# Softmax sums on four column groups at once, two pairs summed by the vector engine, filler matmuls at the start and moved weight steps in an attention and mixing kernel

## The chip, the cores and the metric

The kernel runs on one core of a Trainium2 chip. A core has a matmul engine (PE, with its weight loads shown as PEld), a vector engine (DVE), a scalar engine (ACT), GpSimd (POOL) and a queue engine that issues the transfers here (SP). The metric is the device time of one execution in microseconds; of several runs the median counts, and less is better. Instruction times come from a profile of one execution.

## The reference

For each of 8 batches, softmax attention with a soft cap over 12 heads of 64 channels and 448 positions, and then a mixing layer on the 768 channels:

```python
scores = scale * np.matmul(q, k.transpose(0, 1, 3, 2))
scores = cap * np.tanh(scores / cap)
scores = scores - np.max(scores, axis=-1, keepdims=True)
attn = np.exp(scores)
attn = attn / (np.sum(attn, axis=-1, keepdims=True) + 1e-09)
x = np.matmul(attn, v)           # heads side by side: (8, 448, 768)

theta = x @ w_theta
zr, zi = x * np.cos(theta), x * np.sin(theta)
u = x + einsum(w_tok_r, zr) + einsum(w_tok_i, zi)
out = u + np.maximum(u @ w_ch, 0.0)
```

All arrays are float32. Where the cap is at most 64 the kernel leaves out the maximum (the branch that runs here); the other branch, `general`, is in the program and is not taken.

## The kernel before

**Pairs and stages.** Two heads make a pair, so a batch has 6 pairs and the program 48. It goes through stages `s`. Stage `s` computes the scores of pair `s` in two halves (`qk_half`: 448 keys as four blocks of 112 rows, two blocks to a half), each half followed on ACT by a tanh (L195) and later by an exponential in place (`exp_half`, L201). In the same stage the pair before, `k = s - 1`, is multiplied by its values (`av`, L233), copied out by ACT (L236), and its exponentials are summed over the keys (`sums`). Every second pair the sums are inverted (`invert`, a DVE reciprocal, L275) and spread over the rows by transfers; two or three stages later `norm` multiplies the attention output by them.

**Sums.** The sum over keys is a matmul with a block of ones 32 columns wide (`sum_pair`, L248), so that each head of two pairs has 32 rows of one PSUM tile `r`: rows 0 and 32 for the even pair, 64 and 96 for the odd one. Pairs below `DIRECT = 10` sum all four blocks on PE, pair by pair. For later pairs DVE adds the four blocks first (`add_half`, L223 and L226), and PE sums the result of both pairs in one go.

**Buffers.** The scores have one PSUM tile of four banks, so the next half's scores wait for the tanh of this half. All else on PE shares four tiles of one bank each (tag "m"): attention output, sums, theta, transposes, mixing and channel results, one after another.

**First stages.** Stages 0 to 7 (`FIRST = 8`) have attention alone, and beside it the weights are prepared: each 128-row piece of `w_theta` (th), `w_tok` (tk) and `w_ch` (ch) is loaded (`>th2`), scaled on ACT (`*th2`, L101) and split by seven DVE instructions into a rounded part and a rest (`th2`, L106 to L115; for ch pieces the copy into the rounded part is ACT's, L111). The table `WEIGHTS` says after which step of which stage each word stands. The th and ch pieces share two staging buffers `g_sb0` and `g_sb1`, which theta uses later too. ch pieces 2 to 5 are prepared in stages 11 to 13.

**Later stages.** From stage 8 on each group of six stages, parts 0 to 5, also runs one batch of the mixing layer by `part_scripts`: theta (L299 to L301), sine and cosine, rotation (L323), transposes on PE (`transp`, L332, with the split of the result on ACT, L333, and DVE, L334), mixing over positions (`mix`, L341 to L343), and the channel product (`chan`). In float32r three products replace one, with split operands `xs`, `us`, `zh` and `zl`. From pair 14 on (`WHOLE`) the scores use split operands too, made by `prep` on DVE (L178, L179) one stage ahead.

**Order.** Nothing is scheduled by a tool: every engine works through its instructions in the order in which the code issues them, and semaphores hold an instruction until its operands are there and its output's buffer is free. SP issues the transfers in program order as well, and one that waits holds up those behind it.

Of the kernel before, what the change touches and what calls it, by code (L numbers as in the profile page):

```python
# [28 lines left out]
DIRECT = 10  # L29
# [5 lines left out]
def softcap_attn_then_spectral_mix(ctx, tc, qk2, v, cap, w_theta, w_tok, w_ch, ident, outT):  # L35
# [47 lines left out]


    class Split:
# [14 lines left out]
        def scale(self):  # L100
            nc.scalar.activation(self.hw, self.hw, AF.Copy, scale=2.0**-112)  # L101

# [136 lines left out]
    def sum_pair(k, r, halves=(0, 1)):  # L239

        if k in pst:
            addends = [(pst.pop(k), True, True)]
        else:
            addends = [(pt[k, c // 2][:, c % 2], c == 0, c == NCH - 1) for c in range(NCH) if c // 2 in halves]
        for a, start, stop in addends:
            for hh in range(2):
                i = 2 * (k % 2) + hh
                nc.tensor.matmul(r[32 * i : 32 * i + 32, :S], ones_sb, a[:, hh, :], start=start, stop=stop)  # L248

    def sums(k, halves=(0, 1)):  # L250

        direct = k < DIRECT or state["general"]
# [4 lines left out]
        if direct:
            if state["general"] and 0 not in halves:
                return
            sum_pair(k, state["r"], halves)  # L260
        else:
            sum_pair(k - 1, state["r"])
            sum_pair(k, state["r"])
# [223 lines left out]
```

## Time and profile before

| | |
|---|---|
| median of 3 runs | 981.16 us (980.04 to 984.58) |
| the profiled execution, time | 981.55 us |
| its span, first to last instruction | 979.7 us |
| PE busy | 953.9 us, 97% of the span |
| DVE busy, ACT busy | 631.6 us, 597.4 us |
| mean granted PE clock | 0.995 |
| stage 8's first theta matmul starts | 96.68 us |

The span leaves out 1.85 us before the first and after the last instruction. "PE busy" counts from a matmul's start to its modelled end, and matmuls overlap; so 97% says that PE seldom stands still, not that it works at its peak. A float32 matmul of the program shows as two records in the trace (float32r ones and transposes as one), so 8 records of scores are four matmuls of the program. In a timeline a row gives the start, the time from the first start to the last end of the records that it merges, the engine, the line, the operation, output and inputs, the count, and in brackets the idle time before it with what ended that.

### The profile page before, as it was taken

The page shows a single profiled execution, that of the slowest core. Times are in us where ns is not written, and L with a number is a line of the kernel's source. Part 1 is how long each engine was busy: PE and PEld are TensorE (multiplying, and loading weights), DVE is VectorE, ACT ScalarE, POOL GpSimd, SP SyncE. Part 2 cuts the span into 40 slices and gives each one's busy share as a digit, 9 for nine tenths or more (in the row PEclk, how much of TensorE's full clock was granted, in tenths as well). Part 3 has the DMA queues.
Part 4 walks back from the last instruction along what each step waited for, and adds up shares of the span by engine and source line. Part 5 has one row for each costly group of instructions (what it writes and reads, how often), then busy time and mean ns, then how long its engine had stood idle before and what let it go on. Part 6 is the DMA issues. An engine that isn't in the chain of part 4 may idle for free.

```text
span 979.7 us, 12717 instructions
## 1 busy us (share of the span) xinstructions
PE 953.9 (97%) x5192; PEld 693.5 (71%) x5192; DVE 631.6 (64%) x865; ACT 597.4 (61%) x615; POOL 0.4 (0%) x6
## 2 busy tenths in 40 slices
PE   6999999989999999999999999999999999999997
PEld 2333667657787787777677767876877777789897
DVE  5788665885865658557676567665586566763541
ACT  5887676466954677555876469636784567642520
POOL 0000000000000000000000000000000000000000
PEclk9999999999999999999999999999999999999999
DMA  6654221322102211032111321122211330102001
GB/s 221 196 186 127 66 69 39 121 98 85 48 29 76 79 54 48 30 104 76 38 48 36 106 67 46 49 68 75 66 48 29 86 93 29 29 1 76 1 1 60
DMA packets 30739, 68.68 MB, mean 70 GB/s; under 512 B 4304, under 2 KB 16720, under 8 KB 30672
## 3 DMA queue, kind: packets, MB, share of 16 engines
q1 hardware_dynamic: 30672, 67.78, 22.7%
q8 instruction: 43, 0.70, 0.3%
q14 instruction: 24, 0.20, 0.1%
HBM read 45.74 MB, written 11.01 MB: 58 GB/s over the span
## 4 chain that ended last, share of the span: by engine, by line
PE 78%; DVE 10%; ACT 9%; DMA 2%; issue 1%; SPq 0%; DVEq 0%
PE a L233 13%; PE s L193 12%; PE mx L341 6%; PE mx L342 6%; PE mx L343 6%; PE ch L299 6%; PE ch L301 6%; PE ch L300 6%; PE th L299 4%; PE th L300 4%; PE th L301 4%; PE r L248 3%; ACT p L195 3%; PE t L332 3%; DVE ri L275 2%; ACT p L201 1%
## 5 line engine op out<-in xcount | busy, mean ns | idle before, releaser
L195 ACT ACTIVATE p<-s,qscale 112x1792 f32<-112x1792 f32 x96 | 168.7, 1757 | 171.2 <-PE s L193 171.1
L201 ACT ACTIVATE p<-p,cap_sb 112x1792 f32<-112x1792 f32 x96 | 170.6, 1790 | 0.5
L233 PE MATMUL a<-p,v 112*64 112x448 f32 x768 | 155.5, 547 | 0.0
L341 PE MATMUL mx<-wtk_h,zh 128*128 128x448 f32 x336 | 126.3, 376 | 1.8 <-DVE zl L334 1.8
L342 PE MATMUL mx<-wtk_l,zh 128*128 128x448 f32 x336 | 122.9, 366 | 0.0
L343 PE MATMUL mx<-wtk_h,zl 128*128 128x448 f32 x336 | 122.9, 366 | 0.0
L233 PEld LDWEIGHTS a<-p,v 112*64 112x64 f32 x768 | 51.0, 137 | 87.9 <-issue 78.5
L299 PE MATMUL ch<-us,wch_h 128*128 128x448 f32 x288 | 107.2, 372 | 0.0
L299 PE MATMUL th<-xs,wth_h 128*128 128x448 f32 x288 | 106.9, 371 | 0.0
L301 PE MATMUL ch<-us,wch_l 128*128 128x448 f32 x288 | 105.6, 367 | 0.0
L300 PE MATMUL ch<-us,wch_h 128*128 128x448 f32 x288 | 105.5, 366 | 0.0
L300 PE MATMUL th<-xs,wth_h 128*128 128x448 f32 x288 | 105.4, 366 | 0.0
L301 PE MATMUL th<-xs,wth_l 128*128 128x448 f32 x288 | 105.3, 366 | 0.0
L226 DVE TENSOR_TENSOR ps<-ps,p 112x896 f32<-112x896 f32 x76 | 82.7, 1088 | 1.3
L275 DVE RECIPROCAL ri<-r 128x448 f32<-128x448 f32 x24 | 70.9, 2954 | 14.8 <-PE r L248 14.8
L312 DVE SCALAR_TENSOR_TENSOR g_sb<-g_sb 128x448 f32<-128x448 f32 x48 | 30.0, 624 | 72.6 <-ACT g_sb L311 72.2
L334 DVE TENSOR_TENSOR zl<-t,zh 128x512 fp32r<-128x512 f32 x96 | 55.2, 617 | 24.9 <-ACT zh L333 24.9
L341 PEld LDWEIGHTS mx<-wtk_h,zh 128*128 128x128 f32 x336 | 63.2, 188 | 7.7 <-DVE zl L334 3.0
L352 DVE SCALAR_TENSOR_TENSOR x<-ch,x 128x448 f32<-128x448 f32 x48 | 29.8, 621 | 59.0 <-PE ch L301 59.0
L343 PEld LDWEIGHTS mx<-wtk_h,zl 128*128 128x128 f32 x336 | 63.1, 188 | 5.3
L342 PEld LDWEIGHTS mx<-wtk_l,zh 128*128 128x128 f32 x336 | 63.2, 188 | 4.8
L344 DVE TENSOR_TENSOR x<-mx,x 128x448 f32<-128x448 f32 x48 | 29.9, 623 | 52.9 <-PE mx L343 52.3
(71 smaller groups left out, 1411.6 us busy)
## 6 DMA issues: line engine op xcount, KB each, us to landing
qk_sb<-in_qk SPq DMA_DIRECT2D x35, 448.0 KB, 3.3
v<-in_v SPq DMA_DIRECT2D x48, 224.0 KB, 2.5
bc<-ri SPq DMA_DIRECT2D x96, 112.0 KB, 2.3
out_dram<-x SPq DMA_DIRECT2D x48, 224.0 KB, 2.0
qk<-in_qk SPq DMA_DIRECT2D x13, 448.0 KB, 3.3
g_sb<-in_wth SPq DMA_DIRECT2D x6, 768.0 KB, 5.1
g_sb<-in_wch SPq DMA_DIRECT2D x6, 768.0 KB, 5.3
swk_raw<-in_wtok SPq DMA_DIRECT2D x7, 448.0 KB, 4.2
```

The source lines that it names most:

```text
L193: nc.tensor.matmul(sp[:CP, i, hh, :S], kk[k][rows, 1, ks], qq[k][rows, 0, :], start=n == 0, stop=n == len(products) - 1)
L195: nc.scalar.activation(pp, sp[:CP, :, :, :S], AF.Tanh, scale=qscale[:CP])
L201: nc.scalar.activation(pp, pp, AF.Exp, scale=cap_sb[:CP])
L226: nc.vector.tensor_tensor(pst[k], pst[k], pt[k, 1][:, i], op=ALU.add)
L233: nc.tensor.matmul(acc[hh * D : (hh + 1) * D, :S], va[:, hh, c, :], pt[k, c // 2][:, c % 2, hh, :], start=c == 0, stop=c == NCH - 1)
L275: nc.vector.reciprocal(ri, r[:, :S])
L299: nc.tensor.matmul(acc[:, :S], wh[:, j, ms], t[:, 0, :], start=j == 0, stop=False)
L300: nc.tensor.matmul(acc[:, :S], wh[:, j, ms], t[:, 1, :], start=False, stop=False)
L301: nc.tensor.matmul(acc[:, :S], wl[:, j, ms], t[:, 0, :], start=False, stop=j == NJ - 1)
L341: nc.tensor.matmul(acc[:, :S], zh[:, c, :], wtk_h[:, c, :], start=c == 0, stop=False)
L342: nc.tensor.matmul(acc[:, :S], zh[:, c, :], wtk_l[:, c, :], start=False, stop=False)
L343: nc.tensor.matmul(acc[:, :S], zl[:, c, :], wtk_h[:, c, :], start=False, stop=c == NC2 - 1)
```

## The change

**Fillers.** A new `fill(n)` issues n matmuls of the ones block with itself, 112 columns each, into a PSUM tile that nobody reads. 8 stand ahead of the branch on the cap, 2 ahead of the first scores, 8 between the two halves of stage 0 and 10 behind them.

**Sums of the first batch.** For pairs 0 to 5 the sums of an even pair are no longer issued in its own stage; they are issued with those of the odd pair after it, block by block, so that matmuls for all four row groups of `r` stand next to each other. The exponentials of an even pair must live one stage longer: those of pairs 0, 2 and 4 get buffers of tag "xhl", which the split operands `xs` and `us` use later. For that `split_x` now takes one buffer for two of its operands (3 buffers twice as large in place of 6). Pairs 6 and 7 are summed as before.

**Pairs 8 and 9.** `DIRECT` goes from 10 to 8, so DVE adds the four blocks of these pairs, three instructions each, and PE sums them together in stage 10.

**Weight steps.** Pieces th0 to th3 and ch2 are scaled on DVE (`#`, `vscale`) and not on ACT; ch2's copy into the rounded part also goes to DVE. tk6 is split in stage 9 and not at the end of stage 8. ch2 is split early in stage 11, and the load of ch4 into the same buffer follows it there; the load of ch3 stays at the end of stage 11.

**Part 2.** In part 2 of every batch `invert` and `prep` move behind the first script entry, the transposes and the split of piece 1.

```diff
-DIRECT = 10
+DIRECT = 8
+
+FILL = {"before the branch": 8, "first scores": 2, "half": 8, "slot": 10}
...
+    def fill(n):
+
+        t = psM.tile([P, 512], F32, tag="m", name=f"fill{len(fills)}")
+        fills.append(t)
+        for _ in range(n):
+            nc.tensor.matmul(t[:32, :CP], ones_sb, ones_sb[:, :1].broadcast_to([CP, CP]), start=True, stop=True)
...
+        def vscale(self):
+            nc.vector.tensor_scalar_mul(self.hw, self.hw, 2.0**-112)
...
-            steps["ch", m] = Split(room_g(m), w_ch[m], wch_h[:, :, ms], wch_l[:, :, ms], True)
+            steps["ch", m] = Split(room_g(m), w_ch[m], wch_h[:, :, ms], wch_l[:, :, ms], m != 2)
...
-        (0, "a"): "*th0", (0, "b"): "th0 >th2", (0, "c"): "*th1 *tk0", (1, "b"): "tk0 >tk2 th1 >th3",
-        (2, "a"): "*th2", (2, "b"): "th2 >th4", (2, "c"): "*tk1", (3, "a"): "*th3", (3, "b"): "tk1 >tk3 th3 >th5",
+        (0, "a"): "#th0", (0, "b"): "th0 >th2", (0, "c"): "#th1 *tk0", (1, "b"): "tk0 >tk2 th1 >th3",
+        (2, "a"): "#th2", (2, "b"): "th2 >th4", (2, "c"): "*tk1", (3, "a"): "#th3", (3, "b"): "tk1 >tk3 th3 >th5",
...
-        (8, "b"): "tk5", (8, "c"): "*tk6 tk6 *ch1", (9, "a"): "ch1", (10, "c"): ">ch2", (11, "a"): "*ch2", (11, "c"): "ch2 >ch4 >ch3", (12, "b"): "*ch3 ch3 >ch5", (12, "c"): "*ch4 ch4", (13, "b"): "*ch5 ch5",
+        (8, "b"): "tk5", (8, "c"): "*tk6 *ch1", (9, "a"): "tk6 ch1", (10, "c"): ">ch2", (11, "a"): "#ch2 ch2 >ch4",
+        (11, "c"): ">ch3", (12, "b"): "*ch3 ch3 >ch5", (12, "c"): "*ch4 ch4", (13, "b"): "*ch5 ch5",
...
+    def apart(k):
+        return k < NP and k % 2 == 0
...
-        pp = pt[k, half] = wk.tile([CP, 2, 2, S], F32, tag="p", name=f"p{k}_{half}", bufs=3)
+        if apart(k):
+            pp = wk.tile([CP, 2, 2, S], F32, tag="xhl", name=f"p{k}_{half}", bufs=3)
+        else:
+            pp = wk.tile([CP, 2, 2, S], F32, tag="p", name=f"p{k}_{half}", bufs=3)
...
-        for a, start, stop in addends:
-            for hh in range(2):
-                i = 2 * (k % 2) + hh
-                nc.tensor.matmul(r[32 * i : 32 * i + 32, :S], ones_sb, a[:, hh, :], start=start, stop=stop)
+        for tiles, start, stop in addends:
+            for k, a in zip(ks, tiles):
+                for hh in range(2):
+                    i = 2 * (k % 2) + hh
+                    nc.tensor.matmul(r[32 * i : 32 * i + 32, :S], ones_sb, a[:, hh, :], start=start, stop=stop)
...
-        direct = k < DIRECT or state["general"]
+        alone = state["general"] or NP <= k < DIRECT
...
+        sum_pairs((k,) if alone else (k - 1, k), state["r"], halves)
...
-        t = wk.tile([P, 2, S], F32R, tag="xhl", name=f"{name}{b}_{j}", bufs=6)
+        if j % 2 == 0:
+            state["xhl"] = wk.tile([P, 2, 2, S], F32R, tag="xhl", name=f"{name}{b}_{j}", bufs=3)
+        t = state["xhl"][:, j % 2]
...
-                if not start:
+                if not start and part != 2:
                     invert(k)
...
-            if WHOLE <= s + 1 < NS:
+            if WHOLE <= s + 1 < NS and (start or part != 2):
                 prep(s + 1)
...
+                if part == 2 and i == 0 and not start:
+                    if 0 <= k < NS:
+                        invert(k)
+                    if WHOLE <= s + 1 < NS:
+                        prep(s + 1)
```

ACT in stages 0 and 1, up to the copy of the first attention output; `p0_0` is half 0 of pair 0, `g_sb0` holds th0, `g_sb1` th1 and `swk0_raw` tk0. Before:

```order
L195 ACTIVATE p0_0_121<-s0_0_120,qscale_70 112x1792
L101 ACTIVATE g_sb0_86<-g_sb0_86 128x768
L201 ACTIVATE p0_0_121<-p0_0_121,cap_sb_67 112x1792
L195 ACTIVATE p0_1_132<-s0_1_131,qscale_70 112x1792
L201 ACTIVATE p0_1_132<-p0_1_132,cap_sb_67 112x1792
L101 ACTIVATE g_sb1_87<-g_sb1_87 128x768
L101 ACTIVATE swk0_raw_114<-swk0_raw_114 128x448
L195 ACTIVATE p1_0_152<-s1_0_151,qscale_70 112x1792
L201 ACTIVATE p1_0_152<-p1_0_152,cap_sb_67 112x1792
L236 COPY x0_168<-a0_159 128x448
```

and with the change:

```order
L219 ACTIVATE p0_0_133<-s0_0_132,qscale_70 112x1792
L225 ACTIVATE p0_0_133<-p0_0_133,cap_sb_67 112x1792
L219 ACTIVATE p0_1_153<-s0_1_152,qscale_70 112x1792
L225 ACTIVATE p0_1_153<-p0_1_153,cap_sb_67 112x1792
L112 ACTIVATE swk0_raw_123<-swk0_raw_123 128x448
L219 ACTIVATE p1_0_184<-s1_0_183,qscale_70 112x1792
L225 ACTIVATE p1_0_184<-p1_0_184,cap_sb_67 112x1792
L260 COPY x0_200<-a0_191 128x448
```

The two scalings of th pieces are gone from ACT; that of tk0 stays.

PE from the attention output of pair 0 on to the sums of stage 2 (`a` is attention output, `r` sums, `s` scores; each row is a run of the program's matmuls). Before:

```order
L233 MATMUL a0_159<-p0_1_132,v0_110 64x448 x4
L248 MATMUL r0_172<-p0_0_121,ones_sb_83 32x448 x4
L193 MATMUL s1_1_177<-qk1_112 112x448 x4
L248 MATMUL r0_172<-p0_1_132,ones_sb_83 32x448 x4
L193 MATMUL s2_0_209<-qk2_138 112x448 x4
L233 MATMUL a1_218<-p1_0_152,v1_129 64x448 x4
L233 MATMUL a1_218<-p1_1_178,v1_129 64x448 x4
L248 MATMUL r0_172<-p1_0_152,ones_sb_83 32x448 x4
L193 MATMUL s2_1_235<-qk2_138 112x448 x4
L248 MATMUL r0_172<-p1_1_178,ones_sb_83 32x448 x4
```

and with the change:

```order
L257 MATMUL a0_191<-p0_1_153,v0_119 64x448 x4
L217 MATMUL s1_1_204<-qk1_121 112x448 x4
L217 MATMUL s2_0_232<-qk2_170 112x448 x4
L257 MATMUL a1_241<-p1_0_184,v1_150 64x448 x4
L257 MATMUL a1_241<-p1_1_205,v1_150 64x448 x4
L273 MATMUL r1_254<-p0_0_133,ones_sb_83 32x448 x2
L273 MATMUL r1_254<-p1_0_184,ones_sb_83 32x448 x2
```

Stage 1 has no sums; in stage 2 the two pairs alternate, two matmuls each: the last two rows come once more for the half's second block, and the same again for half 1 behind the scores.

DVE in part 2 of batch 1 (stage 16), where `ri15` is the inverse of the sums, `hi17` and `lo17` the split operands of the next scores, and `zl1_1` the split of the transposes of piece 1. Before:

```order
L323 TENSOR_TENSOR g_sb0_86<-g_sb0_86,x8_734 128x896
L275 RECIPROCAL ri15_1770<-r15_1765 128x448
L178 CAST hi17_1793<-qk_sb_85 128x896
L179 TENSOR_TENSOR lo17_1794<-qk_sb_85,hi17_1793 128x896
L334 TENSOR_TENSOR zl1_1_1799<-t1_1_0_1800,zh1_1_1798 128x512
L334 TENSOR_TENSOR zl1_1_1799<-t1_1_4_1807,zh1_1_1798 128x384
L344 TENSOR_TENSOR x6_534<-mx1_0_1815,x6_534 128x448
```

and with the change:

```order
L346 TENSOR_TENSOR g_sb0_86<-g_sb0_86,x8_760 128x896
L357 TENSOR_TENSOR zl1_1_1805<-t1_1_0_1806,zh1_1_1804 128x512
L357 TENSOR_TENSOR zl1_1_1805<-t1_1_4_1813,zh1_1_1804 128x384
L296 RECIPROCAL ri15_1819<-r15_1784 128x448
L193 CAST hi17_1827<-qk_sb_85 128x896
L194 TENSOR_TENSOR lo17_1828<-qk_sb_85,hi17_1827 128x896
L367 TENSOR_TENSOR x6_564<-mx1_0_1834,x6_564 128x448
```

The two splits stand ahead of the reciprocal and the casts.

More of the change, by code (lines that the diff above doesn't have):

```diff
@@ L78, in softcap_attn_then_spectral_mix @@
     g_sb = [const.tile([P, 3, 2, S], F32, name=f"g_sb{i}") for i in range(2)]
+    def fill(n):
[3 more added lines that the diff above has]
+            nc.tensor.matmul(t[:32, :CP], ones_sb, ones_sb[:, :1].broadcast_to([CP, CP]), start=True, stop=True)
+    fills = []
     def load_consts():
@@ L152, in weights @@
             step = steps[word[-3:-1], int(word[-1])]
-            {">": step.load, "*": step.scale}.get(word[0], step.split)()
+            {">": step.load, "*": step.scale, "#": step.vscale}.get(word[0], step.split)()
     hi, lo, vt, pt, pst, bc = {}, {}, {}, {}, {}, {}
@@ L181, in prep @@
             load_qk(k + 1)
+    def apart(k):
+        return k < NP and k % 2 == 0
     def qk_half(k, half):
         sp = psS.tile([P, 2, 2, 512], F32, tag="s", name=f"s{k}_{half}")
-        pp = pt[k, half] = wk.tile([CP, 2, 2, S], F32, tag="p", name=f"p{k}_{half}", bufs=3)
+        if apart(k):
+            pp = wk.tile([CP, 2, 2, S], F32, tag="xhl", name=f"p{k}_{half}", bufs=3)
+        else:
+            pp = wk.tile([CP, 2, 2, S], F32, tag="p", name=f"p{k}_{half}", bufs=3)
+        pt[k, half] = pp
         for i in range(2):
@@ L237, in av, with sum_pairs @@
         X[k // NP, k % NP] = x
-    def sum_pair(k, r, halves=(0, 1)):
-        if k in pst:
-            addends = [(pst.pop(k), True, True)]
-        else:
-            addends = [(pt[k, c // 2][:, c % 2], c == 0, c == NCH - 1) for c in range(NCH) if c // 2 in halves]
-        for a, start, stop in addends:
-            for hh in range(2):
-                i = 2 * (k % 2) + hh
-                nc.tensor.matmul(r[32 * i : 32 * i + 32, :S], ones_sb, a[:, hh, :], start=start, stop=stop)
+    def sum_pairs(ks, r, halves=(0, 1)):
+        if ks[0] in pst:
+            addends = [([pst.pop(k) for k in ks], True, True)]
+        else:
+            addends = [([pt[k, c // 2][:, c % 2] for k in ks], c == 0, c == NCH - 1) for c in range(NCH) if c // 2 in halves]
+        for tiles, start, stop in addends:
[3 more added lines that the diff above has]
+                    nc.tensor.matmul(r[32 * i : 32 * i + 32, :S], ones_sb, a[:, hh, :], start=start, stop=stop)
     def sums(k, halves=(0, 1)):
-        direct = k < DIRECT or state["general"]
-        if not direct and k % 2 == 0:
+        alone = state["general"] or NP <= k < DIRECT
+        if not alone and k % 2 == 0:
             return
-        if (k % 2 == 0 or not direct) and 0 in halves:
+        if state["general"] and 0 not in halves:
+            return
+        if (k % 2 == 0 or not alone) and 0 in halves:
             state["r"] = psM.tile([P, 512], F32, tag="m", name=f"r{k}")
[L257 to L263, printed above, removed]
+        sum_pairs((k,) if alone else (k - 1, k), state["r"], halves)
     def invert(k):
@@ L384, in pipeline @@
             start = s < FIRST
+            if s == 0:
+                fill(FILL["first scores"])
             if live:
                 qk_half(s, 0)
+            if s == 0:
+                fill(FILL["half"])
             if start:
@@ L404, in pipeline @@
                 qk_half(s, 1)
+            if s == 0:
+                fill(FILL["slot"])
             if 0 <= k and start:
@@ L441, in softcap_attn_then_spectral_mix @@
         steps[step].load()
+    fill(FILL["before the branch"])
     wide = nc.values_load(wide_cap[:1, :1], min_val=0, max_val=1)
```

## The prediction

> **What bounds the kernel now.** I read the page's busy shares first, then who waits for whom on PE (engine, line, what it waited for; us in total, times, longest), then the timeline of the stretches with waits.
>
> ```profile
> PE s L193 <- ACT p L195: 8.9, 10, 2.8
> PE s L193 <- DMA qk_sb<-in_qk: 5.3, 1, 5.3
> PE t L332 <- DVE zl L334: 4.6, 6, 0.8
> ```
>
> PE is busy nearly all the span (the table above), and these three rows are most of its idle time. So time goes only where PE gets less work, or where one of these waits goes. The second stretch to read is a plain early stage:
>
> ```profile
> 27.86 3.23 PE L233 MATMUL a<-p,v 112*64 112x448 f32 x16
> 31.02 1.70 PE L248 MATMUL r<-p,ones_sb 112*32 112x448 f32 x8
> 32.64 1.76 PE L193 MATMUL s<-qk 64*112 64x448 f32 x8
> 34.45 1.76 ACT L195 ACTIVATE p<-s,qscale 112x1792 f32<-112x1792 f32 x1 [1.82 <-PE s L193]
> 36.24 1.79 ACT L201 ACTIVATE p<-p,cap_sb 112x1792 f32<-112x1792 f32 x1
> 37.95 2.48 PE L233 MATMUL a<-p,v 112*64 112x448 f32 x12
> ```
>
> One stage lasts 10.09 us (27.86 to 37.95), and these rows are a closed loop: attention output, half the sums, second scores, tanh, exponential, and with that the next attention output. PE looks full, but a sum taken out behind the attention output shortens the loop by its whole 1.62 us (31.02 to 32.64); one taken out behind the second scores shortens nothing, as ACT works meanwhile.
>
> **A. The start, to stage 2's first scores (26.17).**
>
> ```profile
> 5.30 3.17 PE L193 MATMUL s<-qk_sb 64*112 64x448 f32 x8 [5.30 <-DMA qk_sb<-in_qk]
> 8.51 1.75 ACT L195 ACTIVATE p<-s,qscale 112x1792 f32<-112x1792 f32 x1 [2.82 <-PE s L193]
> 10.17 0.90 ACT L101 ACTIVATE g_sb<-g_sb 128x768 f32<-128x768 f32 x1
> 10.32 1.76 PE L193 MATMUL s<-qk_sb 64*112 64x448 f32 x8 [1.86 <-ACT p L195]
> 14.43 2.82 PE L193 MATMUL s<-qk 64*112 64x448 f32 x8 [2.35 <-ACT p L195]
> 16.89 0.59 ACT L101 ACTIVATE swk_raw<-swk_raw 128x448 f32<-128x448 f32 x1
> 26.17 1.76 PE L193 MATMUL s<-qk 64*112 64x448 f32 x8 [0.23 <-ACT p L195]
> ```
>
> Equal scores take 3.17, 1.76 and 2.82 us. The windows say why (stretch, length, PE, PEld, DVE, ACT, POOL busy, granted clock, DMA share, GB/s):
>
> ```profile
> 8.20:11.60 3.40, 1.54 (x10) 0.64 (x8) 0.44 (x1) 3.09 (x3) 0.00 (x0) 1.00 1.02 339
> 11.60:15.00 3.40, 1.05 (x8) 0.38 (x6) 3.26 (x6) 3.37 (x3) 0.00 (x0) 1.00 1.05 337
> 15.00:18.40 3.40, 3.40 (x12) 0.96 (x10) 2.57 (x4) 3.40 (x4) 0.00 (x0) 0.50 0.33 60
> 199.30:202.70 3.40, 0.75 (x4) 0.45 (x6) 3.30 (x5) 2.91 (x3) 0.00 (x0) 1.00 0.02 7
> 202.70:206.10 3.40, 3.40 (x10) 1.80 (x7) 2.29 (x4) 1.44 (x1) 0.00 (x0) 0.50 0.41 135
> ```
>
> After 3.4 us in which PE was busy 1.05 or 0.75 us the clock was halved for the next 3.4 us; after 1.54 us it was not. The fillers work against this. Their price has no row. The nearest is a transpose, 128 columns against their 112:
>
> ```profile
> 128.68 0.93 PE L332 MATMUL t<-ident_sb,g_sb 128*128 128x128 f32 x7
> ```
>
> 0.93 / 7 = 0.13 us a record, two records to a float32 matmul, 56 records in all. Bounds: 0.05 (a sums record, 1.62 / 8 = 0.20, by 112/448 columns) and 0.55 (below, rival 4). At 0.13 the 16 records between the halves take 2.1 us against a gap of 1.86, and the 20 behind them 2.6 against 2.35: late by 0.25 each, if at all. The 20 ahead of the first scores, at half clock, take 5.2 us in a gap of 5.30 that the ones block opens somewhat late: perhaps 0.5 late.
>
> Scores then start at 5.3 to 5.8 and take between 1.76 and 3.17 us. That puts the first tanh between 7.1 and 9.0; I take 7.8 in place of 8.51, under the middle, since the fillers ahead last longer than one 3.4 us window. From there ACT has no th scaling: tanh and exponential twice, at 1.79 us each (34.45 to 36.24), is 7.2 us, tk0 0.6, so the tanh of stage 1 starts at 15.6 (its like stood at 16.89 + 0.5). PE takes up pair 0's attention output when the second exponential ends, at 7.8 + 7.2 = 15.0 and a little, needs 3.16 (27.86 to 31.02) and, with no sums between, 1.69 for the scores; tanh 0.1 later, next scores 1.8 later: 15.1 + 3.16 + 1.69 + 0.1 + 1.8 = 21.9. Against 26.17 that is **4.3 us** less (5.2 if the first scores are at full clock, 1.5 if they are not and all three groups of fillers overrun by 0.7).
>
> **B. Stages 2 to 7.** The loop loses its sums in stages 3 and 5 (1.62 each). In stages 2, 4 and 6 it holds the sums of two pairs. Pairs summed by four row groups already stand in the trace:
>
> ```profile
> 112.74 3.20 PE L248 MATMUL r<-p,ones_sb 112*32 112x448 f32 x16
> 180.42 0.96 PE L248 MATMUL r<-ps,ones_sb 112*32 112x448 f32 x8
> ```
>
> Eight records on four groups take 0.96 us, on two 1.70, so 16 on four take 1.8: 0.2 longer than now. Sum: 2 x 1.62 - 3 x 0.2 = **2.6 us**, not the 9 that PE's work goes down by. Low end: if p operands don't overlap on four groups, 3.2 - 1.6 = 1.6 more in three stages: a loss of 1.6.
>
> DVE must keep up:
>
> ```profile
> 60.00:80.00 20.00, 19.55 (x98) 6.15 (x96) 17.71 (x28) 15.95 (x15) 0.00 (x0) 1.00 0.56 184
> 11.16 0.56 DVE L106 TENSOR_SCALAR g_sb<-g_sb 128x768 int32<-128x768 int32 x1 [7.30 <-ACT g_sb L101]
> ```
>
> 17.7 us in two stages, and 0.56 for a scaling (the row of an equally large instruction; 0.96 is what the others take), is 18.3 against 20.2 - 1.4 = 18.8 for two stages: hidden, barely. DVE also starts some 3 us earlier, as it waited 7.30 us for ACT's first scaling, which hides what the barely leaves; without that cover stage 7 and its ACT copy of ch0 would come late.
>
> **C and D. Pairs 8 and 9.** Stage 9 loses the 3.14 us of pair 8's sums (3.20 less the overlap with the next), stage 10 trades its own for a 0.96 row: 2.25.
>
> ```profile
> L226 DVE TENSOR_TENSOR ps<-ps,p 112x896 f32<-112x896 f32 x76 | 82.7, 1088 | 1.3
> 124.45 0.63 DVE L312 SCALAR_TENSOR_TENSOR g_sb<-g_sb 128x448 f32<-128x448 f32 x1 [7.47 <-ACT g_sb L311]
> 117.68 1.76 ACT L195 ACTIVATE p<-s,qscale 112x1792 f32<-112x1792 f32 x1 [3.29 <-PE s L193]
> ```
>
> The three adds of a pair are 3.3 us of DVE; pair 8's fit in the 7.47 us that DVE idled, pair 9's between two rotations, ahead of the splits. ACT idled 3.29 us ahead of stage 9's second tanh, and the scores now come 3.14 earlier: it can follow, with no slack left. I charge 0.4 for the sine and rotation chain behind it and 0.7 in stage 10, where the reciprocal is late for a mixing product (F). So **2.7** and **1.5** (low ends 1.5 and 0.5, high 3.1 and 2.25).
>
> **E. Stages 11 to 13.**
>
> ```profile
> 187.78 0.91 ACT L101 ACTIVATE g_sb<-g_sb 128x768 f32<-128x768 f32 x1 [2.84 <-DMA g_sb<-in_wch]
> 199.41 0.83 ACT L111 CAST wch_h<-g_sb 128x768 fp32r<-128x768 f32 x1 [4.08 <-DVE g_sb L107]
> 201.95 2.61 PE L193 MATMUL s<-qk 64*112 64x448 f32 x8 [2.83 <-ACT p L195]
> ```
>
> Stage 13's tanh stands on ACT behind the copy at 199.41, and that behind DVE, which works off exponentials that stood behind the scaling at 187.78, which waited 2.84 us for ch3. ch3's load waited on SP behind ch4's, and that for ch2's split. With ch2 split at the start of stage 11, both loads go some 15 us earlier; the chain moves up by 2.84 us, about what PE waited. With the wait goes the halved clock from 202.70 to 206.10, worth 1.7 us. **4.4** (low end 0, if the copies still hold the tanh; high 4.5). ch2's eight instructions on DVE now stand ahead of the splits of piece 4; mixing of piece 3, 4.3 us on PE, covers part.
>
> **F. Part 2 of batches 1 to 6.**
>
> ```profile
> 260.58 2.95 DVE L275 RECIPROCAL ri<-r 128x448 f32<-128x448 f32 x1
> 261.09 0.95 ACT L333 CAST zh<-t 128x512 fp32r<-128x512 f32 x2
> 265.05 1.15 DVE L334 TENSOR_TENSOR zl<-t,zh 128x512 fp32r<-128x512 f32 x2
> 264.43 0.60 PE L332 MATMUL t<-ident_sb,g_sb 128*128 128x128 f32 x4
> 266.26 0.48 PE L341 MATMUL mx<-wtk_h,zh 128*128 128x448 f32 x1
> 270.65 0.93 PE L332 MATMUL t<-ident_sb,g_sb 128*128 128x128 f32 x7
> 271.33 0.45 PE L341 MATMUL mx<-wtk_h,zh 128*128 128x448 f32 x1
> ```
>
> Undisturbed, mixing starts 0.68 us after its transposes (270.65 to 271.33); here 1.83, so 1.15 lost, since the split at 265.05 stands behind the reciprocal. Now the split goes first, 0.6 after ACT's copy at 261.09, and the reciprocal ends at 261.7 + 1.1 + 2.95 = 265.75. But four PSUM tiles go round: the next mixing product takes that of the sums, due at 265.11, and waits 0.65 for the reciprocal. Gain 0.5 a batch, six times: **2.9** (0 if the split is held elsewhere; 6.9 if nothing waits).
>
> **At nothing.** The th scalings of stages 2 and 3 leave ACT where it idled 1.82 us a stage anyway (34.45). tk6's split, now behind theta on DVE, is first read by the mixing of stage 10, and DVE idles 7.47 us between. The reciprocal's four transfers and the next load of scores operands move on SP with their DVE work, by the 1.2 us of the split; they are wanted two stages and one stage later, and no PE row waits for them now. The exponentials in "xhl" free their buffer by sums that stand on PE ahead of the scores that need it. `xs` buffers in pairs wait for the last products of two pieces in place of one, three more of at most 0.45 us (271.33), and are wanted only after a whole attention block.
>
> **Sum.** 4.3 + 2.6 + 2.7 + 1.5 + 4.4 + 2.9 = 18.4 us, off the profiled 981.55, which is 0.4 above the median: **963**.
>
> **Rivals.** 1. *The clock drops in the new gaps.* In stages 1, 3 and 5 PE now waits 1.9 us for a tanh, so 3.4 us can hold as little as 1.5 us of work: at the edge of what stayed at full clock above (1.54). A drop costs up to 1.7 us; with two, 966. The Trainium skill ("TensorE: Matmul & The Clock Gate", "HAM oscillation — how this bites in real kernels") has it that only gaps over some 3.4 us matter; by that rule this rival is void, the fillers are idle and E is worth 1.7 less, which makes 964.7. The trace disagrees: gaps of 2.35 and 2.83 us were followed by the halved clock. 2. *Four groups don't overlap* when they read exponentials as they are; B turns into -1.6: 967. For it: no row has it. Against: the 0.96 row has the same shapes and its own operand for each pair. 3. *DVE becomes the bound*: at 18.3 of 18.8 us any further 0.4 us (a scaling at 0.96, the adds at both rotations) passes on to ACT's copies in stages 7 and 9; half of A and B and all of D lost, 4 to 6 us: 968. 4. *Slower: fillers don't overlap.* They all write the same 32 rows of one tile. If each waited for the one before, a record would take its whole 0.55 us (155.5 us for the row below, 547 ns a record), 56 x 0.55 = 31 us, of which the three gaps cover 9.5: 22 - 18.4 gives 985; it turns at 0.5 us a record.
>
> ```profile
> L233 PE MATMUL a<-p,v 112*64 112x448 f32 x768 | 155.5, 547 | 0.0
> ```
>
> Against it: 16 such records into one tile took 3.2 us (27.86), 0.2 each. 5. *Without E*: the moved ch2 split holds DVE in stage 11, the wait just moves: 967.5.
>
> **Numbers.** 963 holds 0.62, rival 1 0.12, 2 0.07, 3 0.11, 4 0.04, 5 0.04. The range 957 to 971 takes in rivals 1, 2, 3 and 5 and, below, F's and A's high ends. About 0.5%, 5 us, is what a measurement here tells from no change: faster 0.94, same 0.03 (rival 3 at its worst), slower 0.03 (most of rival 4).
>
> **What would show it.** A: stage 2's scores near 22 us, no row at 0.50 clock before 30. B: stages 3 and 5 near 8.5 us, 2, 4 and 6 near 10.3; stage 8's theta 7 us earlier than 96.68. C, D: no r row in stage 9, one of about 0.96 in stage 10. E: no PE wait near 190 and no halved clock there. F: PE's waits in part 2 moved from transposes to mixing, behind L296. Wrong it would be if fillers stretch past 0.3 us a record, or if theta of stage 8 waits for a weight split.

## The result and the profile after

The changed kernel takes 965.37 us (median of 4, 964.41 to 966.53) against 981.59 us (median of 4, one run more than above, 980.04 to 984.58). The ratio is 0.9834, its 95% interval 0.9813 to 0.9855: 1.7% faster. The forecast was 963, in a range of 957 to 971. The profiled execution took 966.27 us, its span 964.5 (before 981.55 and 979.7).

The start of each attention output (the first of its 16 records) is a milestone that both traces have. Set side by side, they show where the time went:

| from the milestone before to | before | after | change | predicted |
|---|---|---|---|---|
| stage 2's attention output | 27.86 | 24.80 | -3.06 | A: -4.3 |
| stage 8's | 88.70 | 82.42 | -3.22 | B: -2.6 |
| stage 10's | 131.23 | 122.28 | -2.67 | C: -2.7 |
| stage 11's | 156.19 | 146.17 | -1.07 | D: -1.5 |
| stage 14's | 217.84 | 203.58 | -4.24 | E: -4.4 |
| stage 46's, past five of the six part-2 stages that F speaks of | 829.39 | 813.10 | -2.03 | F: -2.9 in six |
| end of the last matmul, the sixth among them | 974.5 | 959.4 | +1.1 | F, and nothing given back |

The waits of the changed kernel's PE answer to the first three rows of the prediction (what waited, for what, us in total, times, longest):

```profile
PE s L217 <- ACT p L219: 6.7, 7, 1.9
PE mx L364 <- DVE ri L296: 3.6, 7, 0.5
PE mx L364 <- DVE zl L357: 1.8, 1, 1.8
PE t L355 <- DVE g_sb L346: 0.3, 1, 0.3
```

The wait of the first scores for their operand (5.3 us) is filled. The transposes no longer wait for the split (4.6 us before); in its place mixing waits for the reciprocal, 0.5 us in each of seven part-2 stages (stage 10 and the six of F). The waits for a tanh fell from 8.9 to 6.7 us.

The timeline of the start, with rows left out between:

```profile
4.48 0.95 PE L87 MATMUL fill<-ones_sb 112*32 112x112 f32 x4 [0.34 <-issue]
5.36 3.33 PE L217 MATMUL s<-qk_sb 64*112 64x448 f32 x8
8.62 2.33 PE L87 MATMUL fill<-ones_sb 112*32 112x112 f32 x16
8.74 1.75 ACT L219 ACTIVATE p<-s,qscale 112x1792 f32<-112x1792 f32 x1 [3.06 <-PE s L217]
10.88 1.76 PE L217 MATMUL s<-qk_sb 64*112 64x448 f32 x8
12.57 2.14 PE L87 MATMUL fill<-ones_sb 112*32 112x112 f32 x20
14.64 1.76 PE L217 MATMUL s<-qk 64*112 64x448 f32 x8
16.33 3.23 PE L257 MATMUL a<-p,v 112*64 112x448 f32 x16
23.10 1.76 PE L217 MATMUL s<-qk 64*112 64x448 f32 x8 [1.85 <-ACT p L219]
```

The fillers did not bring the first scores to full clock: 3.33 us, as slow as before (3.17). The next 16 fillers start at half clock, last 2.33 us, and the second scores start at 10.88, when the tanh that they had waited for before (8.74 + 1.75 = 10.49) has been over for 0.39 us. From there on all scores take 1.76; the slow ones of 2.82 us at 14.43 are gone.

Stage 2 and the start of stage 3, where stage 2 has the sums of two pairs and stage 3 has none:

```profile
24.80 3.23 PE L257 MATMUL a<-p,v 112*64 112x448 f32 x16
27.95 1.71 PE L273 MATMUL r<-p,ones_sb 112*32 112x448 f32 x16
29.59 1.76 PE L217 MATMUL s<-qk 64*112 64x448 f32 x8
31.40 1.75 ACT L219 ACTIVATE p<-s,qscale 112x1792 f32<-112x1792 f32 x1 [2.49 <-PE s L217]
33.21 1.76 PE L217 MATMUL s<-qk 64*112 64x448 f32 x8 [0.21 <-ACT p L219]
```

Sixteen records of sums on four row groups take 1.71 us, where eight on two took 1.70 before. So stage 2 is as long as it was (24.80 to 34.90, 10.10 us, before 10.09), and stage 3 is 8.46 us.

Stage 9 has no sums any more, and stage 10 those of both pairs in one row. The first row here is in stage 9:

```profile
119.70 0.95 PE L355 MATMUL t<-ident_sb,g_sb 128*128 128x128 f32 x7 [0.27 <-DVE g_sb L346]
...
125.43 1.38 PE L273 MATMUL r<-ps,ones_sb 112*32 112x448 f32 x8
```

The sums of stage 10 take 1.38 us and not the 0.96 of the row that the prediction showed for eight records on four groups. The weight load for pair 9's records waits 0.29 us for DVE, whose last two additions for pair 9 run from 123.61 to 125.82.

In stage 13 PE's wait of 2.83 us at 201.95 is gone. The copy ahead of that tanh on ACT (it is ch4's) still waits 4.09 us for DVE, but the tanh behind it comes early enough:

```profile
186.64 0.84 ACT L125 CAST wch_h<-g_sb 128x768 fp32r<-128x768 f32 x1 [4.09 <-DVE g_sb L121]
187.38 1.76 ACT L219 ACTIVATE p<-s,qscale 112x1792 f32<-112x1792 f32 x1
189.19 1.76 PE L217 MATMUL s<-qk 64*112 64x448 f32 x8
```

The 1.5 us given back at the end (1.1, and F's sixth part of 0.42) are a halved clock of 3.41 us in batch 7, which the kernel before did not have in its profile. It follows a wait of mixing for the last split:

```profile
906.83 0.47 PE L364 MATMUL mx<-wtk_h,zh 128*128 128x448 f32 x1 [1.83 <-DVE zl L357]
```

The windows (stretch, length, busy time of PE, PEld, DVE, ACT and POOL, granted clock, DMA share, GB/s):

```profile
20.11:23.52 3.41, 1.55 (x10) 0.48 (x8) 3.31 (x5) 2.73 (x4) 0.00 (x0) 1.00 0.59 189
...
904.17:907.58 3.41, 1.58 (x12) 1.29 (x11) 2.82 (x6) 3.41 (x7) 0.00 (x0) 1.00 0.00 0
907.58:910.99 3.41, 3.41 (x11) 3.02 (x10) 1.72 (x3) 1.33 (x2) 0.00 (x0) 0.50 0.00 0
```

The same wait of 1.83 us was in the kernel before as well (at 923.54), and no halved clock followed it. How it lies in the windows of 3.41 us in which the clock changes is a likely difference, but not the whole of it, as the last section shows. The stretch of 20.11 to 23.52, with the wait of 1.85 us at 23.10, did not cost anything in this execution.

### The profile page after: what moved, and what is told of

It is laid out like the page before. It is cut to its first block, busy times and chain, and to the rows that moved or that the text cites. A ratio compares the mean times of both kernels' runs of the same rounds, so it can differ in the third digit from the quotient of the medians.

```text
span 964.5 us, 12776 instructions
## 1 busy us (share of the span) xinstructions
PE 945.6 (98%) x5224; PEld 697.3 (72%) x5224; DVE 640.8 (66%) x877; ACT 590.5 (61%) x609; POOL 0.4 (0%) x6
## 4 chain that ended last, share of the span: by engine, by line
PE 88%; DVE 6%; ACT 4%; issue 1%; POOL 0%; POOLq 0%
PE a L257 15%; PE s L217 14%; PE mx L364 6%; PE mx L366 6%; PE mx L365 6%; PE th L322 6%; PE ch L322 6%; PE ch L324 6%; PE th L323 6%; PE ch L323 6%; PE th L324 6%; PE t L355 3%; PE r L273 3%; ACT p L219 2%; DVE ri L296 2%
## 5 line engine op out<-in xcount | busy, mean ns | idle before, releaser
L250 DVE TENSOR_TENSOR ps<-ps,p 112x896 f32<-112x896 f32 x80 | 87.0, 1087 | 1.4
L322 PEld LDWEIGHTS ch<-us,wch_h 128*128 128x128 f32 x288 | 54.1, 188 | 9.6 <-issue 4.6
```

The costliest lines, as they stand in the source:

```text
L250: nc.vector.tensor_tensor(pst[k], pst[k], pt[k, 1][:, i], op=ALU.add)
L322: nc.tensor.matmul(acc[:, :S], wh[:, j, ms], t[:, 0, :], start=j == 0, stop=False)
```

## The experiments

All are edits of the changed kernel, whose 965.37 us they are compared with. Where an edit adds lines, line numbers in the rows are up to two higher. Single executions of one kernel lie up to 4.5 us apart (980.04 to 984.58 for the kernel before), and one part of that is visible: the first scores are at full clock in some profiles and at half clock in others. Another is the halved clock in batch 7: it is in the profiles of the changed kernel, of the run with 448 unused bytes and of the one with the scalings on ACT, and in no other. And the kernel before, run again beside the experiments, took 981.90 to 982.45 us in the median. So milestones are compared too, not only times, and a difference of about 1 us between two medians says little.

### No fillers

```diff
-FILL = {"before the branch": 8, "first scores": 2, "half": 8, "slot": 10}
+FILL = {"before the branch": 0, "first scores": 0, "half": 0, "slot": 0}
```

> The changed kernel without its 28 filler matmuls, all else as it is. Theory 1 (fillers keep the clock up): the 3.4 us from about 11.6 to 15 hold 0.5 us of the second half's scores and at most 1.1 of stage 1's, at the edge of what was followed by a halved clock (1.05) and what was not (1.54); a row of 0.50 clock follows, stage 1's scores take 2.8 us and not 1.76, and the attention output of pair 0 is slower too: 0.7 to 1.7 us longer, 966 to 967. Theory 2 (fillers are only a cost here, as stage 1's scores come earlier anyhow without the scalings on ACT): no halved row before 30 us; the first tanh starts at 8.5 and not 8.74, the second scores with its end and not 0.39 later, stage 2's attention output at 24.2 and not 24.80: 964.8, 0.6 us shorter.

966.7 us (965.58 to 968.82). PE at the start:

```profile
5.24 3.33 PE L219 MATMUL s<-qk_sb 64*112 64x448 f32 x8 [5.24 <-DMA qk_sb<-in_qk]
10.43 3.33 PE L219 MATMUL s<-qk_sb 64*112 64x448 f32 x8 [1.85 <-ACT p L221]
15.61 3.33 PE L219 MATMUL s<-qk 64*112 64x448 f32 x8 [1.85 <-ACT p L221]
18.87 4.46 PE L259 MATMUL a<-p,v 112*64 112x448 f32 x16
23.26 1.76 PE L219 MATMUL s<-qk 64*112 64x448 f32 x8
```

Neither theory had this: the clock did not drop, it stayed at half until 21 us. Stage 2's attention output starts at 28.57, 3.8 us later than with fillers. By this profile the fillers are worth 3.8 us, by the medians 1.3, and the times of the two kernels overlap; the kernel before, without any, had its second scores at full clock at 10.32. So in this execution the fillers would have helped, and what they are worth on average is not settled.

### Wide fillers

```diff
+    wide_sb = const.tile([CP, CP], F32, name="wide_sb")
...
-            nc.tensor.matmul(t[:32, :CP], ones_sb, ones_sb[:, :1].broadcast_to([CP, CP]), start=True, stop=True)
+            nc.tensor.matmul(t[:CP, :CP], wide_sb, wide_sb, start=True, stop=True)
```

> The same 28 fillers, but each with a block of ones 112 columns wide as its weights and 112 rows out, in place of 32. Theory 1 (the clock's gate weighs how much of the array works, so the narrow fillers counted for too little): the clock is released before the first scores end, these take 1.8 to 2.6 us and not 3.33, the first tanh starts at 7.2 to 8.0 and not 8.74, and stage 2's attention output 0.7 to 1.5 us earlier than 24.80: about 964.3. Theory 2 (the gate looks at something else, or the fillers come too late for it): the first scores take 3.3 us again, full clock from 9.9 on, no change within 0.2 us.

957.42 us (957.16 to 957.64), 8 us less. But the start is the same: first scores 3.33 us at 5.51, stage 2's attention output at 24.79. So theory 2 held for the fillers, and the 8 us come from elsewhere. From stage 8 on nearly every stage is 0.1 to 0.2 us shorter (stage 14 17.88 against 18.08, stage 15 17.74 against 17.94). There the theta and channel products follow each other every 200 ns and not every 204. The only other thing that the edit did was to move all tiles that lie behind the new block by its 448 bytes a partition. The next four runs take that up.

### 448 unused bytes, narrow fillers

```diff
     ones_sb = const.tile([CP, 32], F32, name="ones_sb")
+    pad_sb = const.tile([P, 112], F32, name="pad_sb")
     ident_sb = const.tile([P, P], F32, name="ident_sb")
```

> The changed kernel with its narrow fillers, and with one more block of 448 bytes a partition in on-chip memory that nothing reads; it lies where the wide block of ones lay, so all tiles behind it (identity, scores and exponentials, xs, us, zh, zl) have the addresses of the kernel with wide fillers, and the weights theirs of both. Layout theory (the products of theta, channels and mixing follow each other faster when their operands lie 64 bytes off a multiple of 128): theta and channel products 200 ns apart and not 204, mixing 202.3 and not 203.6, about 0.2 us less in each stage from 9 on, 957 to 958. Filler theory (the wide fillers did it): 204 ns again, 965.4.

957.59 us (955.54 to 959.03). The third products of stage 14's theta, every third row of the timeline, from the changed kernel:

```profile
209.56 0.36 PE L324 MATMUL th<-xs,wth_l 128*128 128x448 f32 x1
...
215.68 0.36 PE L324 MATMUL th<-xs,wth_l 128*128 128x448 f32 x1
```

and with the unused bytes:

```profile
208.94 0.36 PE L326 MATMUL th<-xs,wth_l 128*128 128x448 f32 x1
...
214.94 0.36 PE L326 MATMUL th<-xs,wth_l 128*128 128x448 f32 x1
```

Both fences show the first and the last of 11 such rows, so 30 products in 6.12 us, 204 ns each, against 30 in 6.00, 200 ns. The duration in the row, 0.36, is the same; only the distance of the starts tells it. The unused bytes alone bring the whole gain of the wide fillers, so it was not the fillers.

### 64 bytes ahead of the weights, 64 or 128 behind them

```diff
+    pad_sb = const.tile([P, 16], F32, name="pad_sb")
     wth_h = const.tile([P, NJ, DM], F32R, name="wth_h")
```

and, for the two others, `pad_sb` with 16 or 32 words in the place that it has in the run with 448 bytes.

> The changed kernel with 64 unused bytes a partition ahead of the weights, so that weights and all other tiles move by 64 bytes and keep their distances. Theory 1 (the address of the 448-column operand counts by itself, whatever the weights' is): theta and channel products 200 ns apart as with wide fillers, and mixing too, whose 448-column operand is now also 64 bytes off: 2736 products x 4 ns = 10.9 us less, about 955. Theory 2 (it is the distance between the loaded block and the 448-column operand): all three as in the changed kernel, 204 ns, 965.4.

> 64 unused bytes a partition behind the weights, so that identity, scores, xs, us, zh and zl move by 64 against the weights (448 before). Theory 1 (what counts is whether loaded block and 448-column operand lie apart by a multiple of 128 bytes): theta and channel products 200 ns apart, as with 448. Theory 2 (the whole distance counts, or its remainder to something larger than 128, 448 having hit a good one): 204 ns or a third value.

> The same with 128 bytes. Theory 1: the remainder to 128 is as in the changed kernel again, so 204 ns. Theory 2: any distance other than the old one may do, 200 ns or a third value.

Mean distance of the starts of consecutive products, over all groups of the trace (864 theta, 864 channel and 1008 mixing products; each group's first product and the few distances over 240 ns left out; the figures are good to 0.2 ns):

| kernel | weights moved by | tiles behind them moved by | theta | channel | mixing | time |
|---|---|---|---|---|---|---|
| before | | (other tiles) | 203.9 ns | 203.8 | 203.8 | 981.59 us |
| the change | 0 | 0 | 203.9 | 203.9 | 203.8 | 965.37 |
| 64 bytes ahead | 64 | 64 | 203.9 | 203.9 | 203.9 | 964.42 |
| 64 bytes behind | 0 | 64 | 202.2 | 202.2 | 200.0 | 958.86 (one execution) |
| 128 bytes behind | 0 | 128 | 203.2 | 203.2 | 202.9 | 962.85 (one execution) |
| 448 bytes behind | 0 | 448 | 200.1 | 200.1 | 202.1 | 957.59 |

Moving weights and data together changes nothing, moving data against weights does. So neither address counts by itself; what counts is how the two lie to each other, theory 2 of the first of the three. It is not just whether the distance is a multiple of 128 bytes: 64 and 448 give different values, and 128 a third one. So theory 1 of the other two falls. With 448 bytes, 1728 x 3.8 ns + 1008 x 1.7 ns = 8.3 us if every distance shrinks; the gain is 7.8 by the medians and 7.2 by the two profiles. Which bits of the distance count stays open, and so does the reason. Mixing, where the block that is loaded is `zh` or `zl` and the 448-column operand a weight, has its best value at another distance than theta. Setting the two apart was not tried.

### Only the casts behind the transposes

```diff
-                if not start and part != 2:
+                if not start:
                     invert(k)
...
                 if part == 2 and i == 0 and not start:
-                    if 0 <= k < NS:
-                        invert(k)
                     if WHOLE <= s + 1 < NS:
                         prep(s + 1)
```

> In part 2 the reciprocal goes back to its old place ahead of the transposes of piece 1; only the two casts for the next scores stay behind them. Theory 1 (the term F of the prediction: the split was late by the reciprocal and the casts together, and the reciprocal alone still leaves it in time): in batch 1 the reciprocal runs from 246.4 to 249.4 and the splits from there to 250.6, before the mixing of piece 1 can use them; PE's wait of mixing for the reciprocal (3.6 us in 7 places) is gone, part 2's stage takes 22.2 us and not 22.90, 0.7 in each of six batches and as much in stage 10: 4.4 to 5.1 us shorter, about 961. Rival (the reciprocal alone holds the split up): PE waits for the split as in the kernel before, the stage is back at 23.3 and the time 2.5 us longer, 968.

959.85 us (959.34 to 960.69), 5.5 less. DVE and PE in part 2 of batch 1:

```profile
245.98 2.95 DVE L296 RECIPROCAL ri<-r 128x448 f32<-128x448 f32 x1
248.85 1.09 DVE L357 TENSOR_TENSOR zl<-t,zh 128x512 fp32r<-128x512 f32 x2
249.84 0.93 PE L355 MATMUL t<-ident_sb,g_sb 128*128 128x128 f32 x7
250.53 0.45 PE L364 MATMUL mx<-wtk_h,zh 128*128 128x448 f32 x1
```

The split is done at 249.9, before mixing can use it, and mixing starts 0.69 us behind its transposes. The wait for the reciprocal is gone from the list, stage 16 takes 22.16 us (22.90 with the change, 23.33 before), stage 10 23.21 (23.89). Over six batches and stage 10 that makes 5.1 of the 5.5 us. The change's own order moved one instruction too many: the whole 1.15 us that term F had counted as lost comes back only if the reciprocal stays where it was.

### Half of the sums one stage earlier

```diff
-                sums(k, (0,) if start else (0, 1))
+                if general or not start or k >= NP:
+                    sums(k, (0,) if start else (0, 1))
...
+            if s < NP and not general:
+                sums(s, (0,))
             if 0 <= k and start:
                 sums(k, (1,))
```

> In stages 1, 3 and 5 the sums of half 0 of both pairs are issued behind the second scores of that stage, in the 1.85 us in which PE waits for the tanh, and no longer in the next stage behind the attention output; PE's matmuls are the same ones. Loop theory (only what stands between attention output and second scores lengthens a stage): stages 2, 4 and 6 fall from 10.10 to 8.46 us, together 4.9; the vector engine, at 18.3 us in two stages against then 16.9, had 4.6 us of idle time ahead of stage 8, so that up to 1.4 comes back: 3.5 to 4.9 us shorter, about 961, theta of stage 8 at 86 to 87 and not 90.40. Rival (PE's work sets the time of these stages): the same matmuls, no change within 0.5 us.

961.66 us (959.82 to 963.8), 3.7 less. PE's matmuls are the same ones; stages 2, 4 and 6 fall from 10.10 to 8.47, 8.59 and 8.47 us, 4.8 together. So the loop theory of term B holds: only what stands between attention output and second scores lengthens a stage. Theta of stage 8 starts at 85.45, 4.95 us earlier than with the change (90.40): these 4.8, another 2.1 because the first scores were at full clock in this profile, less 1.9 that DVE takes back in stage 8 (22.79 against 20.88):

```profile
76.40 0.83 ACT L125 CAST wch_h<-g_sb 128x768 fp32r<-128x768 f32 x1 [2.60 <-DVE g_sb L121]
...
77.14 1.78 ACT L225 ACTIVATE p<-p,cap_sb 112x1792 f32<-112x1792 f32 x1
...
78.98 1.35 PE L257 MATMUL a<-p,v 112*64 112x448 f32 x6 [1.71 <-ACT p L225]
```

ACT's copy of ch0 waits 2.60 us for DVE, the exponential stands behind it, and PE waits 1.71 us for that. This is rival 3 of the prediction, at the copy that it named (ch0's). With the change as it is DVE had the slack.

### ch2 as before

```diff
-            steps["ch", m] = Split(room_g(m), w_ch[m], wch_h[:, :, ms], wch_l[:, :, ms], m != 2)
+            steps["ch", m] = Split(room_g(m), w_ch[m], wch_h[:, :, ms], wch_l[:, :, ms], True)
...
-        (8, "b"): "tk5", (8, "c"): "*tk6 *ch1", (9, "a"): "tk6 ch1", (10, "c"): ">ch2", (11, "a"): "#ch2 ch2 >ch4",
-        (11, "c"): ">ch3", (12, "b"): "*ch3 ch3 >ch5", (12, "c"): "*ch4 ch4", (13, "b"): "*ch5 ch5",
+        (8, "b"): "tk5", (8, "c"): "*tk6 *ch1", (9, "a"): "tk6 ch1", (10, "c"): ">ch2", (11, "a"): "*ch2",
+        (11, "c"): "ch2 >ch4 >ch3", (12, "b"): "*ch3 ch3 >ch5", (12, "c"): "*ch4 ch4", (13, "b"): "*ch5 ch5",
```

> ch2 is scaled and copied by ACT again, split at the end of stage 11, and the load of ch4 follows there; all else as changed. Term E: ch3's load is late again, stage 13's second scores wait 2.8 us for the tanh behind ch3's copy on ACT; stage 13 takes 20.3 us (17.72 + 2.6) if the clock holds and 21.9 if the halved clock follows that gap, as before: 2.6 or 4.2 us more than the changed kernel's 965.4, 968 to 969.6. Rival (the earlier reading of the chain was wrong and pairs 8 and 9 or the order on DVE took the wait away): stage 13 stays at 17.7, no change.

966.9 us, one execution.

```profile
188.88 0.83 ACT L125 CAST wch_h<-g_sb 128x768 fp32r<-128x768 f32 x1 [4.08 <-DVE g_sb L121]
189.62 1.75 ACT L219 ACTIVATE p<-s,qscale 112x1792 f32<-112x1792 f32 x1
...
191.42 1.76 PE L217 MATMUL s<-qk 64*112 64x448 f32 x8 [2.09 <-ACT p L219]
```

The copy at 188.88 is ch4's, not ch3's as expected; ch3's scaling stands before it and waits 2.11 us for its load. PE's wait is back, 2.09 us, and stage 13 takes 19.71 us, 2.0 more, a little under the least that was expected. No halved clock followed this time. So in this one execution the new order of ch2, and with it the earlier load of ch3, is worth 2.0 us. The rest of E's 4.24 is the halved clock of 202.70 to 206.10 and some 0.7 by which the wait was longer in the kernel before, where ch3's load was late by 2.84 and not 2.11 us.

### Scalings of th0 to th3 on ACT

```diff
-        (0, "a"): "#th0", (0, "b"): "th0 >th2", (0, "c"): "#th1 *tk0", (1, "b"): "tk0 >tk2 th1 >th3",
-        (2, "a"): "#th2", (2, "b"): "th2 >th4", (2, "c"): "*tk1", (3, "a"): "#th3", (3, "b"): "tk1 >tk3 th3 >th5",
+        (0, "a"): "*th0", (0, "b"): "th0 >th2", (0, "c"): "*th1 *tk0", (1, "b"): "tk0 >tk2 th1 >th3",
+        (2, "a"): "*th2", (2, "b"): "th2 >th4", (2, "c"): "*tk1", (3, "a"): "*th3", (3, "b"): "tk1 >tk3 th3 >th5",
```

> th0 to th3 are scaled on ACT again; fillers and the rest as changed. Term A's second half: from the first tanh to stage 2's first scores 14.36 us (8.74 to 23.10) become 16.2, as two scalings of 0.9 us stand in the chain of tanh and exponential again; those of th2 and th3 are hidden; stage 8's theta 1.8 us later unless DVE, which starts the first split later, adds to that: 967.2. Rival (the fillers alone brought term A): under 0.5 us.

970.08 us, one execution, and theta of stage 8 at 94.06, 3.7 later. From the first tanh (8.77) to stage 2's first scores (23.37) it is 14.60 us, only 0.24 more than with the change: ACT had the room for th0's and th1's scalings after all. The 3.7 us come from two halved clocks that this execution had in stages 2 and 4, each behind a gap of 1.93 us, of which the first is shown:

```profile
23.37 2.86 PE L217 MATMUL s<-qk 64*112 64x448 f32 x8 [1.93 <-ACT p L219]
```

```profile
20.47:23.89 3.42, 1.49 (x10) 0.51 (x8) 3.28 (x6) 3.39 (x4) 0.00 (x0) 1.00 0.64 177
23.89:27.31 3.42, 3.42 (x12) 1.06 (x10) 3.13 (x4) 2.29 (x2) 0.00 (x0) 0.50 0.40 160
...
40.96:44.37 3.41, 1.48 (x10) 0.49 (x8) 3.31 (x5) 3.38 (x4) 0.00 (x0) 1.00 0.75 214
44.37:47.79 3.42, 3.42 (x10) 0.85 (x8) 2.63 (x4) 2.98 (x3) 0.00 (x0) 0.50 0.43 163
```

This is rival 1. With PE busy for 1.48 or 1.49 us of a window the clock fell, with 1.55 (20.11 above, the same gap in the changed kernel) and 1.54 (the kernel before) it did not. The gap is 1.93 us here and 1.85 there. That the scalings lengthen the gap enough for this is not shown by one execution; how the windows lie differs too. The expected 1.8 us of the scalings themselves were wrong.

### Several edits at once

The first of these has the 448 bytes, the reciprocal back in place and the early sums. The second has one move more:

```diff
-        (5, "c"): "*th5", (6, "b"): "th5 >ch1", (6, "c"): "*tk4", (7, "a"): "*ch0", (7, "b"): "tk4 >tk6 ch0", (7, "c"): "*tk5",
-        (8, "b"): "tk5", (8, "c"): "*tk6 *ch1", (9, "a"): "tk6 ch1", (10, "c"): ">ch2", (11, "a"): "#ch2 ch2 >ch4",
+        (5, "c"): "*th5", (6, "b"): "th5 >ch1", (6, "c"): "*tk4", (7, "a"): "*ch0", (7, "b"): "ch0", (7, "c"): "*tk5",
+        (8, "a"): "tk4 >tk6", (8, "b"): "tk5", (8, "c"): "*tk6 *ch1", (9, "a"): "tk6 ch1", (10, "c"): ">ch2", (11, "a"): "#ch2 ch2 >ch4",
```

> Three of the edits at once: the 448 unused bytes, the reciprocal back in its old place (only the casts stay behind the transposes), and the early sums in stages 1, 3 and 5. If the gains add up: 965.4 - 7.8 (unused bytes) - 5.5 (reciprocal) - 3.0 (sums, of 4.9 in stages 2, 4 and 6, less 1.9 that DVE takes back in stage 8) = 949.1. Rival (a saved wait shows the next one): theta of stage 8 at 85 to 87, but later stages wait for DVE; half of the last two terms lost, 953.

> The same and one move more: tk4's split with the load of tk6 goes from stage 7, ahead of ch0's split on DVE, to stage 8, ahead of tk5's. Theory (in stage 7 ACT's copy of ch0 stands ahead of the exponential and waits 2.6 us for DVE, on which tk4's split of 3.0 us stands ahead of ch0's; that is what took back 1.9 us from the early sums): the wait is gone, stage 8 back at 20.9 us and not 22.8, 1.9 us less than without the move, 947.2. Rival (tk4's split only delays what follows it in stage 8): a wait of the same size at the copies or rotations of stages 8 and 9, no change, 949.

949.18 us (947.23 to 949.47), ratio to the kernel before 0.9670 (0.9655 to 0.9685), and 948.85 us (947.03 to 949.16), ratio 0.9662 (0.9648 to 0.9676). The gains add up as expected for the first (949.1). The second was expected at 947.2, 1.9 us less, and the medians differ by 0.3. Its trace shows the move at work, as ACT's copy of ch0 no longer waits:

```profile
75.69 0.81 ACT L127 CAST wch_h<-g_sb 128x768 fp32r<-128x768 f32 x1
...
77.52 3.23 PE L259 MATMUL a<-p,v 112*64 112x448 f32 x16
```

Stage 8 takes 20.67 us against 22.54. But the two profiled executions last equally long (947.23 and 947.21), as the first's had its first scores at full clock and was 1.9 us ahead by stage 7 for that reason. So the 1.9 us are shown in one stage, not in the time. Both beat the changed kernel by 16 us.

## Why the prediction was right, and which terms were mis-sized

**A, the start: 4.3 predicted, 3.1 measured.** The step that fell short is the first tanh at 7.8, put there since fillers that last over one window of 3.4 us were to bring the clock up within the first scores. It started at 8.74, since these scores ran at half clock throughout; that is 0.9. The same fillers did bring them to full clock (1.76 us) in the profile of the run with early sums, so this term depends on the execution. The fillers between the halves were priced at 0.25 late and were 0.39, as they began at half clock. From the attention output at 16.33 to stage 2's scores at 23.10 it is 6.8 us, as the working had it (15.1 to 21.9). One reason in it was wrong though the sum held: the two scalings on ACT were no part of the gain (0.24 us). What shortened the stretch is the sums that left stage 1, 1.6 us, and the clock.

**B, stages 2 to 7: 2.6 predicted, 3.2 measured.** The loop is right: 8.46 us in stages 3 and 5, and moving sums to the place behind the second scores shortened the other stages by as much. The mis-sized term is the 0.2 us, charged three times, for sixteen records on four groups against eight on two; they take 1.71 against 1.70. With that, 2 x 1.62 = 3.24. A and B together bring stage 8's theta from 96.68 to 90.40, 6.3 us and not the 7 that was to show it. Rival 2 is refuted by the same row.

**C, stage 9: 2.7 predicted, 2.67 measured.** The sine and rotation chain costs what was charged for it: the transposes at 119.70 wait 0.27 us for a rotation on DVE, which is held up by ACT, where the sines stand ahead (DVE idles 4.09 us before 117.07). **D, stage 10: 1.5 predicted, 1.07 measured.** The 0.7 for the late reciprocal was right (0.68 came back with the reciprocal in its old place). The rest is a wait that the prediction put at nothing: pair 9's additions end at 125.82, behind the start of the sums at 125.43, so that the sums take 1.38 us and not 0.96. No run set pairs 8 and 9 back alone; C and D rest on these rows and on the milestones.

**E, stages 11 to 13: 4.4 predicted, 4.24 measured.** As read from the chain; with ch2's old order the wait came back. Some 2.0 to 2.7 are for the order, and the rest is for a halved clock, which did not come back with the old order. How many executions of the kernel before have it is not known, so that part of the number is in part luck.

**F, part 2: 2.9 predicted, 2.45 measured**, 0.42 a batch and not 0.5. The mechanism was as described, with the wait moved to mixing (0.5 us, seven times). Not seen was that the reciprocal alone is short enough to stay.

**Not predicted: 1.5 us given back** through the halved clock in batch 7. With 1.2 in A, 0.4 in D, 0.2 in E and 0.45 in F, less 0.6 in B, that is what parts 963 from the 966.27 of the profiled execution. The halved clock that went in E and the one that came here nearly cancel; two of the changed kernel's four executions took 964.4 us, the profiled one and one more 966.3 and 966.5.

**The rivals.** The first did not come about in the gaps that it named in the profiled execution, but did in the run with scalings on ACT. The third waited one step further, and came with the early sums. The fourth fell: a filler record takes 0.11 us at full clock (2.14 / 20) and 0.2 at half (3.19 / 16 for the first sixteen), not 0.55. The fifth fell with E.

## What to carry to other kernels

In a loop of two engines that wait for each other, ask of each piece of work on which leg it lies. Taken off the leg that the other engine waits for, it counts in full; moved to where its engine waits anyway, it costs nothing, with not one matmul less. When an order is changed to bring one instruction forward, move only what has to give way: here the casts, not the reciprocal. And when an edit that can't have done it makes a kernel faster, look at what it did to the addresses.

## What the hardware showed that was not expected

- **Place of data against weights.** Float32r products of 128x128 by 448 follow each other every 203.9, 203.2, 202.2 or 200.1 ns, depending on the distance in on-chip memory between the block that is loaded and the 448-column operand. Over the 2736 products of this kernel that brought 7.8 us by the medians, nearly half as much as the whole change. Why is open. The duration in a row doesn't show it.
- **The clock falls on a grid of 3.41 us.** In the run with scalings on ACT it was full from 10.24 on and halved at 23.89 and 44.37, 4 and 10 times 3.41 us later, each time for 3.41 us. Gaps of 1.83, 1.93 and 1.93 us were followed by the halved clock, gaps of 1.85 and 2.09 were not. PE's busy time in the window goes some way: windows with 1.48 and 1.49 us were followed by it, those with 1.54 and 1.55 were not. But in batch 7, at the same 1.83 us wait, one with 1.58 was (the changed kernel) and one with 1.59 was not (early sums, 898.57 to 901.99), and with the 448 unused bytes, after a wait of 1.74 us, one with 1.67 was (896.85 to 900.26). What else counts is open. The Trainium skill ("TensorE: Matmul & The Clock Gate", "HAM oscillation — how this bites in real kernels") speaks of gaps over some 3.4 us; here less than 2 us was enough in some executions.
- **When the clock comes up at the start.** In the changed kernel the window from 3.05 to 6.46 had PE busy for 3.07 us with fillers and scores, and the scores went on at half clock until the next window, busy throughout, was over at 9.87; in the kernel before the one from 4.76 to 8.17 had 2.87 us, all scores, and the clock was full after it. In the run with early sums a window of fillers alone (0.87 to 4.28, 3.19 us) was enough. Fillers 112 wide did no better than those 32 wide. What counts was not found.
